# A planned order for a four-layer block, searched anew: the warm-up memset on GpSimd, other start times in the planner, another set of ranks

## The chip, the core and the metric

The kernel runs on one core of one Trainium2 chip. A core has TensorE (PE in the profile; PEld is its weight load), VectorE (DVE), ScalarE (ACT), GpSimd (POOL) and SyncE (SP), which here only issues DMAs. The metric is the device time of one execution in microseconds, the median of several runs. The profile comes from one further execution.

## The reference

Four layers follow each other on `x` (2048 rows, 512 columns, bf16): attention, gated MLP, attention, gated MLP. Each is added to `x`, and each reads the layer norm of `x`.

```python
# attention, H = 32 heads of 16; phi is a feature map, no mask
qkv = x @ wqkv ; q, k, v per head
pq, pk = q @ w_phi, k @ w_phi
phi_q = concat(softmax(pq), softmax(-pq))
phi_k = concat(softmax(pk), softmax(-pk))
kv  = sum over s of phi_k[s]^T v[s] ;  z = sum over s of phi_k[s]
o   = (phi_q @ kv) / (phi_q @ z + 1e-6) ;  return o @ wo
# MLP, F = 1376
gate = relu(x @ W_gate) ; return (gate * (x @ W_up)) @ W_down

x = x + A(layernorm(x)); x = x + B(layernorm(x))
x = x + A(layernorm(x)); x = x + B(layernorm(x))
```

Both attention layers share their weights, and so do both MLPs.

## The kernel before

The rows are cut into 16 tiles of 128 and 4 slabs of 512. All weights and `x` stay in SBUF. The kernel is written as a list of operations with an engine each, made by plain Python functions; a list scheduler then fixes the order of every engine, and the program emits that order with semaphore waits. Each engine runs its own queue strictly in order.

**Names.** A name like `K0.3` is an operation of layer 0, tile 3; layers are 0 (attention), 1 (MLP), 2 (attention), 3 (MLP). By function:

- The set-up (L497 to L608). `warm` (L500, L569) clears a small tile and multiplies it by itself 40 times on TensorE; nothing reads the product. `WkT` and `WqT` (`turn`, L578, matmuls at L585) are transposes of the key and query weights. `Wkp` and `Wqp` (`compose`, L593, L599) multiply them by the block-diagonal matrix `BD` (L572), which holds `w_phi`. "cp" is the copy of such a product from PSUM (L475 on ScalarE, L476 on VectorE).
- `ln` (L610): `stat` and `aggr` on VectorE, `ln` and `rstd` on ScalarE, `y` on VectorE (L639) or GpSimd (L638, after `nmr`), then the transpose `yT`, either a DMA on SP's queue (L653) or a matmul (L648) with a copy `yTcp`.
- `kv_tile` (L660): `K` (L671; the first tile's four matmuls are single operations, L675), two exponentials `expk` (L682), their sums `Z` (L691) or, for ten tiles of layer 0, a half-sum `Zp` on GpSimd (L687) and the rest `Zh` on VectorE (L688); the reciprocal `lZ`, `rZ`; `norm` on VectorE (L700); `V` (L709) and its copy `va`.
- `q_chunk` (L717): `Q` (L724) and two exponentials `expq` (L728).
- `kv_sums` (L736): `kv` (L744) accumulates phi_k and V over the tiles, in bursts of tiles 0-3, 4-7, 8-11, 12-13, 14, 15. `kv0.0.2` is the burst of tiles 8-11 in group 0 of layer 0, and `kv*.2` stands for that burst in all three groups. `kvs` (L752) copies the sums out.
- `attn_tile` (L761): `R` (L777, three groups), `sm` (L791), small products `p`, `den`, `coef` on GpSimd or VectorE (L798, L800, L804), `lden` and `rden` on ScalarE between them (L802, L803), `t` (L814, L819), `o` (L823, or L824 on GpSimd), the transpose `oT` (DMA at L835 or matmul at L830), `wo` (L840), and `xa` (L843), which adds to `x`.
- `glu_slab` (L849): `g` and `u` (L870), relu (L877), `h` (L878), the last 96 columns `rem` (L898), transposed by a DMA `remT` (L907). `down` (L910): `d` in two parts (L924, L926), and `xb` (L932), which adds to `x`.

**The order.** `Program.forward` (L154) simulates the five engines with a fixed duration for each operation and picks at each step, among those that can start, the one with the highest rank. The ranks are stored in the file (`RANKS`, two bytes each, as text), and so is `MOVED`, a list of operations that take the second engine they were written for. The planner lets every engine start at `START` (L53, used at L168) and takes a matmul's duration as it is given; only the first 30 warm-up matmuls are given twice the time of the others (L569). Its own constants act on the order alone: no time of theirs enters the program.

**Order around the change.** SP issues tile 0 of `x`, the key weights in two halves, two more pieces of `x`, the query weights (L559), `x` again and the value weights; GpSimd issues the rest of `x` (L565). TensorE runs 33 warm-up matmuls, the key transposes, `yT0.0`, `Wkp` with seven more warm-up matmuls in between, the four `K0.0`, and then the query transposes.

Of the kernel before, what the change touches and what calls it, by code (L numbers as in the profile page):

```python
# [12 lines left out]
P = 128  # L13

ENGINES = ("sp", "act", "pe", "dve", "pool")
# [36 lines left out]
class Program:  # L52
    SYNC, START = 40.0, 750.0  # L53
# [100 lines left out]
    def forward(self, prio, look=60.0):  # L154


        ops, SYNC = self.ops, self.SYNC
# [10 lines left out]
        free = dict.fromkeys(ENGINES, self.START)  # L168
# [32 lines left out]
        while left:  # L201
            pick = None
            for e in ENGINES:
                f = free[e]
# [4 lines left out]
                for o in ready[e]:  # L209
                    st = o.ready if o.ready > f else f  # L210
# [40 lines left out]
            if o.dma == "tr":  # L251
                free[e] = st + self.TR_ISSUE
                bus = max(bus, free[e]) + o.nbytes
                o.end = bus + self.TR_FIXED
            elif o.dma:
                free[e] = st + o.ii
                bus = max(bus, free[e]) + o.nbytes / self.DMA_BW
                o.end = bus + self.DMA_FIXED
            else:
                free[e] = st + o.ii  # L260
                o.end = st + o.lat
                if e == "pool":
                    pool_end = free[e]
                elif e == "dve" and o.port:
                    port_end = free[e]
# [155 lines left out]
def build_kernel(nc, A_x, A_wqkv, A_w_phi, A_wo, B_x, B_W_gate, B_W_up, B_W_down, out):  # L421
    pr = Program()
    op = pr.op
# [76 lines left out]
    o_warm = op("dve", lambda e: e.memset(wm.ap()[:, 0:128], 0.0), writes=[c_warm], ii=60, lat=100, name="warm")  # L500
# [67 lines left out]
    for k in range(WARM):  # L568
        op("pe", lambda e: e.matmul(pt_w.ap()[:, 0:128], wm.ap()[:, 0:128], wm.ap()[:, 0:128], start=True, stop=True), reads=[c_warm], writes=[r_w], ii=107 if k < 30 else 56, lat=300, name="warm")  # L569
# [436 lines left out]
    '!w2>Ux&|!>HwXv_1qd?;DhMbDD+qc9_XiRP1O*xhEC?V7GzjMhg8@DU@CO(O@dpP8`Uf8fA_o2kU<D`wJqUdSg#|wdY6a8><p<CQ7Y9NJ>jdTl#0MG!J_!B=',  # L1006
    'KnR`$76*_7&jq>%3JB^4r~*U?{|6BW^##`l>j&lsz6Y@civmUn)d!#i=mQ@Ivjz?VtOr>IQwJai{ssdGst2D2pa*3K<pyF0LkKwtm<L1$p#~!ebq8VvWCsZd',
    '&j$bph6Ni3sRv93Qw7=v*9PnayaxsbF$fn3A_yY~Aqb5HE(in&fd)7TF$ORQq6ZlWQU)mqI|zpd90(l+Uk6nO69}dT9SA1~a|ad({Rbon+6Ms${09#R0svSC',
    'P6s9i-Un(2I0rBX6$dW}3<x#|Ee2-?X$J=Y(+8IY4G2jG_Xb-BwFWT<3J2i@bp}TU;s(M63kT5#%m&s5QU^T;%?1t#nFSXH)CM^P&IZc{$_6I~7zbGfum)5H',
    'mj*TluLTVT$OeuE#s+5w6bN4ixd!0|O9r3@Zw7P)KL_yx*ak}gL;>gqSpr@J3<os@D+eA30R&V8t_6ArN(Z3_js@KZ0tapf?gk|YkOo)=*#?^iMF<%OHV1<S',  # L1010
    'qz17DGzR+y;|2=|+Xndug$7OrQwE|2(g%kI0tns)_y+a`fClddC<m_w=?5kV0S8tF-v*fmU<QN+R|Yx;9tY9|&ju+6MFu_xG6o3;y#*u(#|91u;0A~WbOwwD',
    'kp|}mcm_KL@CIE5sRmI74hD$^b_S&es0L{UYz8w1o(6LU1P4I|n*|yNj|K$?lm;ON!v_Bb5C<m(S_U}>V+Ldf#RtI!jRw#KPzKNh9R~FVrUdZ@PX_%4F9#t9',
    'l?Ijs&IRlSYX@To5eI4pB?o#1JO=y(9tPtFmIgcr^9Cse4+m}qIR;Dw90$<{;s=}u^93#j?FJJE83slMt_CUv(gu76BL!#%tOlG0umuVQeh1?P&<3Xk=K?1N',
    '+6CzaG6lE=>IL@&)diddsRT#`90uzK5C#+mF9tgY00y50g9ktc=LH1@*#)}?fCmi+0|xO0z6F#A%LnEK$p>@?zy%Qnat5*mng_N8?*&{3PY25dc?UHIw*`#{',
    'VFc6#M+dM6kOfo)aR-3~Z3lh^1_vMp_68;gLkFz}`Uai{Lk36&JqC~mj|Yqgvj+eOBL;T{B?e{(T?hFEe+L@~<Of9uItQ!;p9ii7YX&d|jt9R7b_d4?nFkOE',
    'r3YFE#|3x=EeA3OiU-OB`3CF<qy>`)w+Dg;-3HtT=>~)cHwVH8%?DQpl?AE>(*~9Yfd_jBO9#~kxCRmjd<3)yod<;n@dVfhwFj*SO$YM_PzSOH!UlW?h6jrW',
    'cn3@e@&{1|+XvwXA_wgU6bDoX?F1VHLIlVMUI!`%sRf${y$7cUeglUC`~{T<%m*_EZwD0!#s@(NyaNXZkq3JQ?gQinv<9^WItZ@^YzMyv_y>pwU<c?2s0Y~x',
    'k_Yq$RtG@`$_GRS?+3XDz625m<pl@?p#?|;<OZq($pp~@>IUEk9S0NzC<br`LI*zu`v<`X1O`<GNd}h(k_OiWng-4XH3X*yDh62xHwNqjG6;qSD+5Lc^#}F@',
    'X#{8m0tRmdDF&Mae+7#Ka0R~v2nN3eKnHOI$^~}^y9O)<8wT<PvIfipHU-26!v*97K?RZpV+9iiOa*WTiv>srmIZAF>jg>#P6ZDJWd>gbQU$;UW(EodO$8qY',
    'g9Y~lga!BoIt4HVNd<5OX9X_>UIW<!{R0vOX$67>O9j#d;sxphD+bX8J_X(cVg`-_H3l>Vd<A0!ECmAvy96l&Nd%k&6$HEjM+IF4b_H7ns0A$qbp%EQl?3Vp',  # L1020
    '`U9W^=mkXu;slHZPX&<#f&)MWE(DnbZ3S`#GX*3A<_07NTm}CHfdeE33IyK;#RUlluLQORSOoe7a|LDvN(03M!2|OIwghwo=>+%$-2{>Z#Reb+Bn0pTlLMCo',
    'v;?;Vh6JkvSp@wAt^}h469kh4Hw8lly93k&A_ZRry9K`k%moPqq6HcRZ3Dvt*aW=<5d@|MCj`g@(**hir3HNl2?bFFKm+~+I|Tm&Q3L}59tC{^eg#_t8U;`U',
    'Wdr*HfCZofBLoWsT?F|AwgdD9Jp!Qv!UJytiUiXEcLYfS<pf3qR|C@nR|FUZECiGT>jM!6as!71Jp(%f!31jrTmy6hTm)<cqXxDIkOPzjy#^Nr7zQ;6JP4)-',
    'Z2|@eJOrc%zz3ZMm<8Vl$p+j7UIu6biUx58*ag-H83lg^kp;2@ss()p(*<`0odsJ4-UYb@O$0&)c?N<8N(Hn9WChU#lLd(fu?4&a)dW@r%>?cT*#s^H>;?M;',
    '-~~hlbOZwj-33(z%>}Ck$pt(G$OZBSodZw>Yz3VJ6$YaPlLp%b!3J0b8wLLaZv^lK0tHnBc?GisD+CA!76ujtm<Bion*!nk90NlFh63aRUjwZIDFgQcU;-Be',
    'E(06|Zv*86ssxAw`vm&~BLkuWzX4AIgaeiW5d)V3I0O|1xdYY(QUfgo)&tiA>;en}ivzO)GXo+5zyrww5(CcyB?Suw9|JK2+61`-5CwSy$^$3^#sgXd6aygx',
    '$O7R4;{rPcbp;It?gW1XMFa)~C<Vp@#{$9xz6LA@9|ed6ZUlA&)C2AXhXwrw!vv262L{{*jReaCKL)S_69u6J#RP-|&je8ew+0Iaqyy#ztOTtDU<6JCI0a<|',
    '$O8=oi3BhNNdsmCvjvO;ECcNWDFPV-Uji5c4g}`|VFJYhvI0f|ngpi=0tCtem;+P;#sbR&@B+>P;sLe+kptNRR01FadjeJjM+6N6-vk;4p91m(-~`_T2?GuT',
    '7z6kM&jCULfdcaa8Uok@83ZB&Jp>2?fdo$jS_JX}^a79qiUMN;a{^=n3j-Acx&&tgeFB&SSpzf!Km?iv+yp-Zvjgt~xCEsGg9DBP+ygWOK?F+#as;0Q2L(3+',
    'M*|cAg9J?m5(FUyn*-<sx&_Gr-UHhM#{|v<0R=$=qy&Hjd;;|Zc?5<77X#e`T>}OKM*?938v>mIsseZdv;yV=hXSbrX9B$eIs^d&rUI@576fwxe*^XcQUoRh',  # L1030
    '?gHTf<pQ|^vI8aq{Q^w_Ed$&Fegv5Vg#yk4(gVN(69Ys8O9C4M!vWR;9s{HTS^^yd-~##rDg<!@jRRx@rvfhoe*z%{QUc-vi30=#paT8^gaWq$0|TQ3f&_^L',
    'd;>8BJOh9O;RFQ*B?AHjr34rR)&#@^cm%ow%L2CpVg$_tHUnz|dITT@HUvHc00lw?5Co3{aRn;{^aNW3Yy)Nk`~sl@ZUfr{00fN!^#eZyGy+iqXau+e^8>&H',
    '`~!Of=mPly#{<a&9|Q*j^aCXXngU`200Z^|g#%Lq?E*mpr~~-}0|c)FGXk*!zXFs3u>)fQrvrcjO9OWUIs-8SY6FM`Pyz)5wE}Dc%mN_+9t5xh1_bZ}Qv!$r',
    'kpW->sRJ(pPXyru)dN-nk^_YVkpjK~ngdn?o&yvDcmt~f-vYV<l>*8D-2(LiRRgR7(E@4$!2;C+Qvf#tP6B5ET>^dp9RPX)0s%(>UIMEGg#l>-J^~K`IRY{S',
    '=>jkUDFCen?*R<}@BnfGTm~iuTLMG`NdZa%mIEIE3IaI*0|58~IRohfZU(#sy#rbWs|R%hs05w`VFwNc4+RYYC<Jf=Xb1ELatEvfUIncKWdt+_GX#qUR|Uoe',
    'wFG1Y3<UfJdjvTI2nBirVFp7376aD;v;$KF9RWW9s{mO5s{uFzr2&rxQUJ^Z;{<yJ@c|+P&ja@Z3<eAZ!~(Sg3IlTl1q9#&G6N6;odKf<*961`q62CK2?A{d',
    '7Xq9FDgjCc0S49q@&o4t?f^&w2LwF<?FG08lmsdR^#c3>W&vgb!~-S*I02>udjZA(eFd)qq5v-gb^}!as|G^^*aDLRVFfM+iUlwOHv!%PNCI~PNB~>{C;|Qh',
    'X#=(bJq5l4n*r|xoB~Y&y8<=>q6BLNiUYg^%m8)*u?Ic`76CT|d;r}5a{w#?asZ430RWx?w*YVg3IRm|!vgUF(*pkj)B?={_yG(85&|6r&;o$~jRB4VIRP#L',
    '000&Oxd7w=xByrKLIddlCIDgrzyXy5egYH(F97EOj{?L1H3QlMP6OKlO#=b~f&w)HnE@>Vx&Zh9>H=y3m;hA)Cjtop`~b57qyeS@>;Rzw=K#q7lL3|iPXXWo',
    'WdQa8WC7O!90ETAtpT_K?*hsJ`vKAd1OqApu>h0-00NKzI|7mbrvUx{fC1S7sR7afJ^+jYUjZNjECHYa;{kF3SORAQy#fRQ5dx3_tN=U#T>ugR-vDy~qXD}C',  # L1040
    ';sCAzi2&&Ve*oJ6p8&=I!~rz{ssXM70Rry;%>lFlhXCFHrU2ytz5!SPnF81WtpE=Livh<0Kmhvyg90-FxB(^sumRcv?EzH+905!LWdaug`T=+VC;(9blmNj2',
    'rvU~6j{(R5(*XGZ{sET(hylC-oB^c(P62@dh5?!ZGyx|7eE{JAHUYE%cmcHmOamSQ+5lhyA^?K`jscngI0EDVO95yBj{w#H%K$9_E&-kZvH;Zq>H$LldI5X^',
    '*Z`jaod9_O5drG~mH=7-S^)V0YXV&X2m!YN5CLNWXaWWS&j57-4gnJYCjlh^#Q{12%>V}h^Z+CQ3jrAbi2`;3^#Dx(qX2pUm;s0YDFF`v&;VfodjNs}00A)q',
    'Py<W?^Z}Uw4+O#hIs!2P#{kX%G6MGjU;zCAMgu$oc><{b;{zcAmjhP;!U6~auL14>9Rjle!U4Si83Nk@$N-T5L;?^3k^=Ss{{bTa(E*<W1Ol)E4FV$q-T@T>',
    'UID-W1p*}k{{RO9vH|P?Q~}ZeMFVaE-vJy1TmkR_TL8rXtN{}O&;tts^8r%<QUNOh)B)rITLGg2l>s6FcL7-eKmv3Dh5#-AMFEWfqyXyz8v&{S>Hs_dD*?6u',
    'HUO9cumFq!HvmNdbpeV2BLQy#-~bl@Pyvzwr2?P;x&h?@-2r9*o&iV!&;f}7Rsn4RaRF=rZUM0YxdEF1z5wz8K>;-Y!vJXkeF0+tFabURe*shgLIFwv%K=6K',
    '6##+(&H;-6H~{7V0RapETmWzYaRLhfVgRTBZU8U<MgSlImjGx0JphCO3IL)3Cj*55Q2=WI@&J<n?EoqO1p(*)+yLkS4+1~|69J3>YXOG=B>*1+7y(xRbpVb4',
    'iU3yvZ2%qsbO7-HWB?!l3;`qpUI6O=c>vh}OaK@FoB+`PfB<Iz`T#lrNdO@Lt^hj#M*tQ80|7$;8vrW+Z~^lGVF6D7{QxuoPyna_egSa+2>=xWy8vnc5CGKx',
    'SOA0o;{f*n)BsKZ6acRPI{|C}Rsh@q83AGe%mK9k9|3Ow8UUdH9s$<?+5s8?<^e1KF9Br%l>iO^LI6Yn!2kvT2mp5gX#f!bb^yNsG5|^d1pqPuK>$Ah8~|Sc',
    'F#r+(yZ{6MGXNw2EdT',  # L1050
)
MOVED = (
    72, 74, 77, 93, 97, 101, 114, 167, 194, 303, 313, 472, 473, 476, 498, 499, 525, 528, 556, 644, 648, 652, 676, 696, 700, 717, 720, 724, 741, 748,
# [60 lines left out]
```

## Time and profile before

| | |
|---|---|
| median of 7 runs | 391.84 us (391.51 to 392.32) |
| the profiled execution | 392.14 us, its span 390.3 us |
| granted TensorE clock over the span | 1.00 |
| first matmul / last instruction's end | 1.22 us / 390.3 us |
| VectorE, ScalarE, GpSimd busy | 290.5, 198.3, 58.4 us |
| DMA transposes to landing, median | 2.5 us (55 of `y`, 28 of `o`) |

The span is from the first to the last instruction; the 1.84 us around it belong to the execution, not to the program's instructions. A row of a timeline gives start, length, engine, line, what is written from what, and a count when equal rows were merged; idle time and who ended it stand in brackets. Busy time of TensorE counts a matmul up to its modelled end, so back-to-back matmuls overlap and only distances between starts tell its pace.

### The profile page before, as it was taken

What the parts mean: (1) busy time and instruction counts of PE and PEld (TensorE: products, weight loads), DVE (VectorE), ACT (ScalarE), POOL (GpSimd) and SP (SyncE); (2) the same over time, 40 slices, a digit from 0 to 9 for tenths busy, and PEclk for the clock granted to TensorE, in tenths of its full rate; (3) what the DMA queues carried; (4) which work ended last, traced back from release to release, by engine and by line L of the source; (5) the groups of instructions that cost most, each with busy time, mean ns of one, the idle gap of its engine ahead of it and who ended that gap; (6) DMA issues with size and microseconds to landing.
All of it is one profiled execution on the core that took longest, in us unless ns stands there. A gap on an engine that the chain in (4) does not pass through costs nothing.

```text
span 390.3 us, 6693 instructions
## 1 busy us (share of the span) xinstructions
PE 380.0 (97%) x2471; PEld 213.7 (55%) x2471; DVE 290.5 (74%) x645; ACT 198.3 (51%) x617; POOL 58.4 (15%) x122
## 2 busy tenths in 40 slices
PE   7999999999999999999999999989999999999996
PEld 6545574787554544444444557567765444444443
DVE  7999978999996678335599996889989853444323
ACT  5899979665453233331269975865455313323100
POOL 2367402223320210000000000131112010000000
PEclk9999999999999999999999999999999999999999
DMA  7642941234242222100210000113233321010002
GB/s 238 177 87 55 335 141 29 53 61 65 40 82 52 44 41 42 27 0 2 53 27 16 13 3 2 28 32 71 50 68 67 55 58 37 29 40 15 1 27 81
DMA packets 60593, 22.89 MB, mean 59 GB/s; under 512 B 51761, under 2 KB 60305, under 8 KB 60561
## 3 DMA queue, kind: packets, MB, share of 16 engines
q1 hardware_dynamic: 57440, 19.35, 22.4%
q10 hardware_dynamic: 2832, 2.08, 1.7%
q0 software_dynamic: 288, 1.05, 0.8%
q8 instruction: 19, 0.31, 0.3%
q14 instruction: 14, 0.11, 0.1%
HBM read 8.44 MB, written 2.10 MB: 27 GB/s over the span
## 4 chain that ended last, share of the span: by engine, by line
PE 78%; ACT 8%; DVE 8%; DMA 4%; issue 1%; SPq 1%; POOL 0%
PE pb L870 34%; PE pb L924 17%; PE pb L840 6%; PE pb L671 4%; PE pb L709 4%; PE pb L724 3%; PE pb L744 3%; PE pb L777 3%; PE pb L898 3%; DVE phik L700 3%; ACT expq L728 3%; ACT phik L682 2%; PE pb L926 2%; DMA Wd<-in_A_wqkv_dram 2%; DVE z L688 1%; DMA oT<-o 1%
## 5 line engine op out<-in xcount | busy, mean ns | idle before, releaser
L877 ACT ACTIVATE gate<-pb 128x512 bf16<-128x512 f32 (+1 forms) x100 | 50.9, 509 | 83.8 <-PE pb L870 83.0
L878 DVE TENSOR_TENSOR hT<-gate,pb 128x512 bf16<-128x512 bf16 (+1 forms) x100 | 57.1, 577 | 41.9 <-PE pb L870 36.6
L870 PE MATMUL pb<-yT,Wu 128*128 128x512 bf16 (+1 forms) x400 | 82.7, 337 | 0.0
L870 PE MATMUL pb<-yT,Wg 128*128 128x512 bf16 (+1 forms) x400 | 81.2, 337 | 0.1
L924 PE MATMUL pb<-Wd,hT 128*128 128x512 bf16 (+2 forms) x330 | 76.6, 373 | 0.0
L870 PEld LDWEIGHTS pb<-yT,Wg 128*128 128x128 bf16 x400 | 38.5, 98 | 30.4 <-ACT gate L877 0.4
L870 PEld LDWEIGHTS pb<-yT,Wu 128*128 128x128 bf16 x400 | 38.6, 98 | 29.9 <-DVE t L814 0.2
L924 PEld LDWEIGHTS pb<-Wd,hT 128*128 128x128 bf16 x330 | 31.5, 98 | 34.8 <-DVE hT L878 0.4
L613 DVE BATCH_NORM_STATS2 stats<-x_sb 128x6 f32<-128x512 bf16 x64 | 43.4, 686 | 0.6
L932 DVE TENSOR_TENSOR x_sb<-x_sb,pb 128x512 bf16<-128x512 bf16 (+2 forms) x33 | 22.0, 668 | 28.0 <-PE pb L926 27.8
L728 ACT ACTIVATE expq<-pb 128x512 bf16<-128x512 f32 x64 | 36.1, 622 | 5.7 <-PE pb L724 5.7
L682 ACT ACTIVATE phik<-pb 128x512 bf16<-128x512 f32 x64 | 35.7, 615 | 1.7 <-PE pb L671 1.6
L814 DVE TENSOR_TENSOR t<-pb,sm 128x384 bf16<-128x384 f32 x64 | 33.9, 549 | 2.1 <-POOL sm L804 1.8
L840 PE MATMUL pb<-wo,oT 128*128 128x512 bf16 x128 | 32.6, 380 | 2.0 <-DMA oT<-o 1.3
L622 ACT ACTIVATE lnv<-mv,eps 128x1 f32<-128x1 f32 (+1 forms) x58 | 17.1, 299 | 30.5 <-DVE mv L614 30.0
L709 PE MATMUL pb<-wv,yT 128*128 128x512 bf16 x128 | 31.2, 379 | 0.0
L724 PE MATMUL pb<-yT,Wqp 128*128 128x512 bf16 x128 | 30.9, 380 | 0.2 <-DVE t L819 0.2
L671 PE MATMUL pb<-Wkp,yT 128*128 128x512 bf16 x124 | 30.2, 380 | 0.0
L639 DVE TENSOR_SCALAR y<-x_sb,mv,rstd 128x512 bf16<-128x512 bf16 x62 | 25.5, 420 | 3.9 <-ACT rstd L624 3.7
L804 POOL TENSOR_TENSOR sm<-sm 128x64 f32<-128x64 f32 x18 | 5.8, 323 | 148.5 <-ACT sm L803 148.5
L791 ACT ACTIVATE sm<-pb 128x48 f32<-128x48 f32 (+1 forms) x96 | 16.4, 221 | 21.6 <-PE pb L777 21.3
L691 DVE TENSOR_REDUCE z<-phik 128x64 f32<-128x1024 bf16 x21 | 24.8, 1203 | 0.6 <-ACT phik L682 0.6
(79 smaller groups left out, 431.5 us busy)
## 6 DMA issues: line engine op xcount, KB each, us to landing
out_dram<-x_sb ACTq DMA_DIRECT2D x15, 128.0 KB, 1.7
Wg<-in_B_W_gate_dram SPq DMA_DIRECT2D x2, 640.0 KB, 7.1
Wu<-in_B_W_up_dram SPq DMA_DIRECT2D x2, 640.0 KB, 8.1
Wd<-in_B_W_down_dram SPq DMA_DIRECT2D x1, 1280.0 KB, 11.5
x_sb<-in_A_x_dram POOLq DMA_DIRECT2D x2, 512.0 KB, 4.7
yT<-y SPq DMA_TRANSPOSE x55, 2.5
Wd<-in_A_wqkv_dram SPq DMA_DIRECT2D x2, 256.0 KB, 3.0
Wd<-in_A_wqkv_dram SPq DMA_DIRECT2D x1, 512.0 KB, 6.8
```

The lines of the kernel that those rows point to most:

```text
L613: op("dve", lambda e, t=t: e.bn_stats(stats[:, t, :], x_sb[:, t, :]), reads=[res("x", t)], writes=[res("st", t)], ii=600, lat=690, name=f" ...
L671: i = e.matmul(kt.ap(), src.ap()[:, ic, c0:c0 + 128], Wkp[:, ic, :], start=(ic == 0), stop=(ic == 3))
L682: op("act", lambda e, s=s: e.activation(ft.ap()[:, s, :], kt.ap(), ACT.Exp, scale=(1.0, -1.0)[s]), reads=[kr], writes=[fr2[s]], ii=477, la ...
L709: i = e.matmul(vt.ap(), src.ap()[:, ic, c0:c0 + 128], wv[:, ic, :], start=(ic == 0), stop=(ic == 3))
L724: i = e.matmul(qt.ap(), Wqp[:, ic, c * 128:(c + 1) * 128], src.ap()[:, ic, :], start=(ic == 0), stop=(ic == 3))
L728: op("act", lambda e, g=g: e.activation(es[g][0].ap(), qt.ap(), ACT.Exp, scale=(1.0, -1.0)[g]), reads=[qr], writes=[es[g][1]], ii=477, lat ...
L814: return e.tensor_tensor(tt_.ap()[:, b, 0:384].rearrange("p (c h d) -> p c h d", h=8, d=16), pt.ap()[:, 0:432].rearrange("p (c w) -> p c w ...
L840: i = e.matmul(wt.ap(), oT_.ap()[:, c, :], wo[:, c, :], start=(c == 0), stop=(c == 3))
L870: i = e.matmul(pt.ap()[:, 0:n], W[:, ic, fc * 128:(fc + 1) * 128], src.ap()[:, ic, a * 128:b * 128], start=(ic == 0), stop=(ic == 3))
L877: op("act", lambda e: e.activation(st_.ap()[:, 0:n], gt.ap()[:, 0:n], ACT.Relu), reads=[gr], writes=[sr], ii=110 + n * .72, lat=230 + n * ...
L878: op("dve", lambda e: e.tensor_tensor(ht.ap()[:, a * 128:b * 128], st_.ap()[:, 0:n], ut.ap()[:, 0:n], ALU.mult), reads=[sr, ur], writes=[h ...
L924: i = e.matmul(pt.ap()[:, 0:n1 - n0], hT[l, s, fc].ap()[:, c:c + 128], Wd[:, fc, n0:n1], start=(fc == 0), stop=False)
```

## The change

It has four parts.

1. The warm-up tile is cleared by GpSimd in place of VectorE. The instruction becomes a memset of 128 two-byte columns in place of 64 four-byte ones, and stands first among GpSimd's own instructions.
2. The planner gets a start time for each engine, and takes matmuls that start before 5600 ns at twice their duration; the warm-up matmuls have one duration.
3. The ranks are replaced.
4. `MOVED` is replaced.

```diff
-    SYNC, START = 40.0, 750.0
+    SYNC, CLOCK = 40.0, 5600.0
+    START = {"sp": 740.0, "act": 760.0, "pe": 400.0, "dve": 800.0, "pool": 310.0}
...
-        free = dict.fromkeys(ENGINES, self.START)
+        free = dict(self.START)
...
-                free[e] = st + o.ii
-                o.end = st + o.lat
+                slow = o.ii if e == "pe" and st < self.CLOCK else 0.0
+                free[e] = st + o.ii + slow
+                o.end = st + o.lat + slow
...
-    o_warm = op("dve", lambda e: e.memset(wm.ap()[:, 0:128], 0.0), writes=[c_warm], ii=60, lat=100, name="warm")
+    o_warm = op("pool", lambda e: e.memset(wm.ap()[:, 0:128], 0.0), writes=[c_warm], ii=60, lat=100, name="warm")
...
-        op("pe", lambda e: e.matmul(pt_w.ap()[:, 0:128], wm.ap()[:, 0:128], wm.ap()[:, 0:128], start=True, stop=True), reads=[c_warm], writes=[r_w], ii=107 if k < 30 else 56, lat=300, name="warm")
+        op("pe", lambda e: e.matmul(pt_w.ap()[:, 0:128], wm.ap()[:, 0:128], wm.ap()[:, 0:128], start=True, stop=True), reads=[c_warm], writes=[r_w], ii=55, lat=240, name="warm")
...
 RANKS = (
...
 MOVED = (
-    72, 74, 77, 93, 97, 101, 114, 167, 194, 303, 313, 472, 473, 476, 498, 499, 525, 528, 556, 644, 648, 652, 676, 696, 700, 717, 720, 724, 741, 748,
...
+    75, 79, 97, 101, 107, 191, 293, 303, 472, 473, 476, 482, 498, 499, 502, 517, 576, 580, 620, 621, 624, 668, 676, 700, 720, 740, 741, 744, 748, 765,
...
```

The ranks are numbers in a packed form; what they do is read from the order that comes out. No operation is added or dropped and every matmul keeps its shape. Of the 2,119 operations these stand differently:

- Engines. 81 operations change their engine. In the set-up and the first kv stage: three `BD` products from GpSimd to VectorE, two `WkT cp` and `yTcp0.0` from VectorE to ScalarE, one `Wkp cp` and one `Wqp cp` from ScalarE to VectorE, `y0.8` and `y0.13` from GpSimd to VectorE, `y0.12` the other way, `va0.6` from ScalarE to VectorE and `va0.8` back. Later: five `va` copies of layer 2, `oTcp0.0`, `oTcp2.0`, `yTcp1.1`, `yTcp2.15` and `yTcp3.0` from ScalarE to VectorE, `yTcp3.1` back, and 56 of the small products `p`, `den`, `coef` and `o` between VectorE and GpSimd, 33 of them to GpSimd.
- TensorE. 35 warm-up matmuls come first (33 before), then the four `WkT`, `yT0.0`, the four `Wkp`, five warm-up matmuls, three of the four `K0.0`, two `WqT`, the last `K0.0`, and the rest. `kv*.2` and what follows it end with `Q0.1.0` ahead of `R0.0.0`, where it stood behind it. Nine `K`, eight `V` and one `Q` of layer 2 run ahead of layer 1's last part `d1.14.1`; before, none did. `wo2.4` moves back behind `wo2.5`; `rem3.2.1`, `wo2.12` and `wo2.14` move too.
- DMA queues. SP's loads keep their order; the transposes follow the new order of `y`, `o` and `rem` (for layer 0: tiles 4, 5, 7, 6, 8, 9, 12, 10, 13, 11, 15, 14). GpSimd's two loads of `x` keep their place behind its sixteen small memsets.

## The prediction

> **What bounds the kernel now.** I read the page first, then busy time by stretch, then TensorE's waits, then single rows.
>
> ```profile
> PE 380.0 (97%) x2471; PEld 213.7 (55%) x2471; DVE 290.5 (74%) x645; ACT 198.3 (51%) x617; POOL 58.4 (15%) x122
> PE 78%; ACT 8%; DVE 8%; DMA 4%; issue 1%; SPq 1%; POOL 0%
> ```
>
> TensorE is the bound, and the chain that ended last is mostly TensorE. A matmul's modelled end overlaps the next one, so I count by starts: four 512-column matmuls start within 0.86 us, 0.216 each. Summed over the 2471 matmuls (0.216, 0.109, 0.0825, 0.0625, 0.058 and 0.056 us for 512, 256, 192, 144, 129 and 128 columns), TensorE's work is 374.9 us. The rest of the span is 1.22 us before the first matmul, 3.28 us from the last start to the end, and 10.95 us of stalls and slow clock in between. The work is the same after the change; only this rest can move. By stretch (each row: length, then busy time of each engine):
>
> ```profile
> 10.00:48.24 38.24, 37.59 (x252) 20.07 (x253) 37.69 (x71) 36.13 (x104) 21.87 (x30) 1.00 0.59 160
> 48.24:69.28 21.04, 19.54 (x180) 12.56 (x181) 16.53 (x43) 17.58 (x60) 3.76 (x9) 1.00 0.30 89
> 69.28:240.00 170.72, 170.72 (x1075) 95.08 (x1076) 132.64 (x277) 81.39 (x251) 16.46 (x29) 1.00 0.19 36
> 240.00:262.74 22.74, 21.05 (x160) 12.79 (x158) 20.18 (x54) 18.39 (x69) 4.76 (x13) 1.00 0.14 25
> 262.74:313.00 50.26, 50.26 (x362) 32.35 (x363) 45.48 (x118) 24.14 (x93) 7.69 (x14) 1.00 0.33 61
> ```
>
> From 69 to 240 and 263 to 313 us TensorE never rests: no order can gain there, only lose. In the first stretch VectorE (37.69 of 38.24) is as full as TensorE. What TensorE waited for:
>
> ```profile
> PE pb L585 <- DMA Wd<-in_A_wqkv_dram: 1.3, 1, 1.3
> PE pb L840 <- DMA oT<-o: 1.3, 1, 1.3
> PE pb L569 <- DVE rowi L502: 1.2, 1, 1.2
> PE pb L898 <- DMA yT<-y: 0.9, 1, 0.9
> PE pb L744 <- DVE phik L700: 0.6, 1, 0.6
> PE pb L648 <- DVE x_sb L843: 0.6, 1, 0.6
> PE pb L840 <- ACT yT L475: 0.5, 1, 0.5
> ```
>
> By starts these are, in order of the list, 1.48 us (at 10.03), 1.46 (wo2.4, at 262.74), the 1.22 at the beginning, 1.03 (rem3.2.1, at 314.32), 0.79 (kv0.0.2, at 48.24), 0.76 (yT1.0) and 0.62 (wo0.3, at 69.28). They are all that the new order can win.
>
> **Part 1: the warm-up memset goes to GpSimd.** The memset took 0.11 us on VectorE behind eight small ones; GpSimd starts at 0.74, and its 512-column memset takes 0.52, so 128 columns cost some 0.15 and the first matmul moves from 1.22 to about 0.95. Its cover:
>
> ```profile
> 1.22 3.57 PE L569 MATMUL pb<-gate 128*128 128x128 bf16 x33 [1.22 <-DVE rowi L502]
> 4.63 0.61 PE L585 MATMUL pb<-ident,Wd 128*128 128x128 bf16 x8
> 3.16 0.47 SPq L559 DMA_DIRECT2D Wd<-in_A_wqkv_dram  x1
> 7.46 1.27 PE L675 MATMUL pb<-Wkp,yT 128*128 128x512 bf16 x3
> 10.03 0.84 PE L585 MATMUL pb<-ident,Wd 128*128 128x128 bf16 x12 [1.30 <-DMA Wd<-in_A_wqkv_dram]
> ```
>
> The warm-up's 33 matmuls start 0.103 us apart, the transposes after it 0.056: the clock rose at about 4.5, 3.3 us after the first. Then everything stands until 10.03, when the query weights (issued at 3.16, 6.8 us to landing) are there. A rule speaks here: the Trainium skill, page "TensorE: Matmul & The Clock Gate", part on the clock gate, says the activity window of some 3.4 us runs free of the kernel. By it the rise may come up to 0.27 us earlier or not at all; by the row, 3.3 us after the start, it comes 0.27 earlier. If it came later, at 5.6 as the planner's new constant has it, the 20 or so real 128-column matmuls in that time would lose 0.055 each, 1.1 us, still under the 1.48 us stall at 10.03. All three give zero. The three BD products that go from GpSimd to VectorE (0.2 us each) lie before 10.03 too.
>
> One thing is not covered. The old order does all four K0.0 matmuls before 10.03; the new one puts two WqT transposes, which wait for 10.03, before the fourth. **+0.22 us** of work is left over, and ScalarE's first exponential moves from 9.06 to about 10.9.
>
> **Part 2: the first kv stage.** VectorE starts at 10.46 with the first WqT copy and does not stop until the last norm ends at 49.99. In the new order its work between these two is the same plus one Wqp copy (0.60 by starts) plus one y (y0.8 and y0.13 come from GpSimd, y0.12 goes there: 0.32): **+0.92 us**. The last norm then ends at about 50.9. GpSimd's half-sums can add to this:
>
> ```profile
> 34.22 2.44 POOL L687 TENSOR_TENSOR t<-phik 128x512 f32<-128x512 bf16 x2 [1.42 <-DVE z L688]
> 35.58 1.63 DVE L700 TENSOR_TENSOR phik<-phik,rz 128x1024 bf16<-128x1024 bf16 x1
> ```
>
> A norm that takes 0.60 took 1.56 by starts, because GpSimd ran. This happened to y0.14, norm0.6 and norm0.7, each second in line after a half-sum had freed a buffer (0.75, 0.96, 0.96). In the new order that place is taken by y0.15, y0.14 and norm0.9: three again, zero. In the new order four norms, not three, follow norm0.11, which kv*.2 waits for: it ends at 50.9 - 2.4 = 48.5. From there 3.7 us of kv matmuls and Q0.1.0 (0.86, which stood behind R0 before) lead to R0.0.0 at 53.1, against 51.95: **+1.15 us** in all, the 0.22 included.
>
> **Part 3: from R0.0.0 to slab 0 of layer 1.** Both orders have 15.1 us of TensorE work from R0.0.0 to the same place; the old one took 17.33 (51.95 to 69.28). Unstalled, the new one is there at 68.2. What is late next is the copy yTcp1.0: following ScalarE's order (21 exponentials of 0.477, four lden/rden pairs, the sm copies; one oTcp and yTcp1.1 now on VectorE) I get its end at 68.6, so rem1.0.0 at 68.7. Bounds are 68.2 and 70.4 (old stalls kept): -1.1 to +1.15. I take **-0.4** for parts 1 to 3 together, near the queue sum's -0.6.
>
> **Part 4: 69 to 240 us.** Nothing to gain. Two edges are tight. wo0.13 to rem1.3.0 has 6.5 us of TensorE work in between; xa, stat, aggr, ln, rstd, y take 2.7 us at best and the transpose 2.5, with 0.2 around the edge: 5.4, 1.1 to spare. K2.14 now ends 4.6 us ahead of kv2.1.4; its two exponentials, Z, lZ, rZ and norm take 3.9. I take **+0.3**, bounds 0 and 0.8.
>
> **Part 5: the second start, 240 to 263 us.** wo2.4 now stands 11.0 us of work behind its R2.4, not 7.1: its 1.46 us go. Late next is wo2.5, 7.9 us behind R2.5 with all four small products on GpSimd (about 2.0 us, against 0.8 on VectorE); that chain sums to 7.4. What the old stall was made of decides:
>
> ```profile
> 258.25 1.19 SPq L835 DMA_TRANSPOSE oT<-o  x1
> q8 instruction: 1, 0.02, 2.8%
> oT<-o SPq DMA_TRANSPOSE x1, 4.4
> ```
>
> The transpose took 4.4 us to land, not the usual 2.5 (median of 28), and in that stretch (259 to 262) one 16 KB instruction block went over the DMA engines; at 311 us, before rem3.2.1, it was 4.0 with a block as well. The Trainium skill, page "Runtime: NRT & Kernel Launch", section "Instruction fetch mechanics", says that blocks of 256 instructions are fetched and that the cost is mostly hidden. By the rule wo2.5 has 0.5 us to spare and the part gains 1.46; by the row a transpose issued within 2 us before a block loses 1 to 1.9. Counting matmuls between the blocks' times in this trace, they come some 124 apart, which puts one just where oT2.5 is in flight. I go by the row: 0.7 us of new stall, **-0.75**, bounds -1.46 and +0.4.
>
> **Part 6: 263 us to the end.** rem3.2.1 waited for y3.10, held up in VectorE's queue and then by a block. Now y3.10 has 23 us and y3.11 7.9, of which 5.9 are needed: **-1.03**. Places with little room are new (d3.3.1 1.4 us behind u3.0.9.2; rem3.3.1 8.2 behind wo2.14; four half-finished sums in PSUM from 334 on): **+0.6**, bounds 0 and 1.5. The tail has the same last four groups: 0.
>
> **Sum:** -0.4 + 0.3 - 0.75 - 1.03 + 0.6 = -1.3 us. The profiled execution took 392.14 (span 390.3 and 1.84 around it); it becomes 390.85. The median of the runs shown, 391.84, is 0.3 lower: **390.6 us**. The bounds add to -3.6 and +2.8; not all meet, so the forecast's own range is 389.5 to 391.2.
>
> **Rivals.** *VectorE becomes the bound of the first 50 us.* For it: 37.69 busy of 38.24 and 0.92 more to do, and y0.7 to y0.11 come 2 to 4 us later than before, with their transposes. Against it: the next part had 2.2 us of stalls to absorb it. Two more meetings with GpSimd (0.96 each) on top of 1.15, absorbed by nothing since ScalarE sets part 3, give +3.1; less some 0.9 that parts 4 to 6 save: 394.0. It decides once R0.0.0 starts after about 54.4. *Stalls only move*: as many tight places meet a block or a queue as before, each some 1 us: 391.8. For it: at most a few of the hundred transposes are critical, and which is chance. *All wins, no new stall*: -1.1, -1.46, -1.03: 388.2; against it speaks every tight edge above. That the order doesn't change is excluded: TensorE's sequence differs from the K0.0 matmuls on.
>
> **Chances.** Forecast 0.42, VectorE 0.32, only moved 0.18, all wins 0.08. What can be told from no change is about 0.2%, 0.8 us: below 391.05 is faster, above 392.6 slower. A tenth of the forecast falls inside the band: faster 0.46, same 0.21, slower 0.33. The range reaches from most of the wins to most of the VectorE case: 388.9 to 393.7.
>
> **What would show it.** First matmul near 0.95 and WqT still at about 10.0; R0.0.0 at 53.1; no stall row on L777 or L840 around 69 us; a stall at wo2.5, none at wo2.4; none at L898 near 310. I am wrong if R0.0.0 is past 54.4, or if the full stretches show stalls over 1 us.

## The result, and the profile after

The new kernel takes **389.97 us** (median of 14 runs, 389.25 to 391.46); the kernel before took 391.84 beside it (35 runs). The ratio is 0.9956, 95% interval 0.9946 to 0.9965: faster by 1.87 us, where 1.3 was forecast. The profiled execution of the new kernel took 388.88 us with a span of 387.1. It is 1.1 us under its own median, so the two profiles differ by more (3.26 us) than the medians do. One row explains the surplus: the first query transpose starts at 8.90 here and at 10.03 before, because the query weights happened to land earlier (5.7 us after their issue instead of 6.8):

```profile
8.90 0.62 PE L587 MATMUL pb<-ident,Wd 128*128 128x128 bf16 x8
```

The load stands at the same place of SP's queue in both kernels, and over all fourteen profiles of this study that transpose starts anywhere from 8.90 to 10.24, in the old and in the new start alike. I therefore count from it where I compare places.

From the page, the busy times and the chain that ended last:

```profile
PE 380.6 (98%) x2471; PEld 214.3 (55%) x2471; DVE 294.5 (76%) x646; ACT 194.9 (50%) x609; POOL 57.4 (15%) x129
PE 79%; DVE 9%; ACT 9%; DMA 1%; issue 1%; POOL 1%; SPq 0%; POOLq 0%
```

DMA has fallen from 4% of the chain to 1%. By stretch (length, then busy time of TensorE, its weight load, VectorE, ScalarE, GpSimd), with the same bounds as before:

```profile
10.00:48.24 38.24, 36.62 (x248) 19.43 (x246) 38.24 (x72) 36.67 (x105) 21.47 (x29) 1.00 0.54 149
48.24:69.28 21.04, 20.91 (x187) 13.16 (x185) 16.68 (x46) 16.17 (x59) 2.63 (x9) 1.00 0.34 104
69.28:240.00 170.72, 170.65 (x1070) 94.23 (x1069) 137.65 (x288) 79.54 (x247) 13.98 (x26) 1.00 0.19 36
240.00:262.74 22.74, 22.56 (x176) 14.59 (x175) 20.31 (x53) 18.02 (x64) 6.44 (x16) 1.00 0.16 32
262.74:313.00 50.26, 50.03 (x340) 30.54 (x338) 40.60 (x95) 20.55 (x79) 7.87 (x21) 1.00 0.28 55
```

VectorE is now busy through the whole first kv stage, 38.24 of 38.24, and TensorE lost a microsecond there; the next stretch gives it back. The fourth stretch, 21.05 of 22.74 before, is now full. TensorE's waits, in answer to the list of before:

```profile
PE pb L746 <- DVE phik L702: 1.3, 1, 1.3
PE pb L571 <- POOL expo L521: 1.0, 1, 1.0
PE pb L673 <- DMA yT<-y: 0.3, 1, 0.3
PE pb L842 <- ACT sm L793: 0.2, 1, 0.2
PE pb L601 <- DVE yT L478: 0.2, 1, 0.2
```

Lines are two higher than before. The waits of `wo` and `rem` for their DMA transposes (L842, L900; 1.3 and 0.9 us before) are gone. A kv burst waited for a norm before too (0.6 us, at `kv0.0.2`); now it waits 1.3 us, one burst earlier, at `kv0.1.1` (L702).

Cut at `R2.0.0`, the first product of the second attention layer, where both orders have done the same work (matmul counts and shapes ahead of it and behind it are equal), the picture is short:

| by starts, us | before | after |
|---|---|---|
| first query transpose to `R0.0.0` | 41.92 | 43.23 |
| first query transpose to the end of stalls around 69 (`wo0.3`, `rem1.0.0`) | 59.25 | 59.23 |
| first query transpose to `R2.0.0` | 228.53 | 228.79 |
| `R2.0.0` to the last matmul | 148.49 | 146.10 |

All of the gain lies behind 238 us. There the work is 144.64 us in both orders, and the stalls fell from 3.85 to 1.46.

### The profile page after: what moved, and what is told of

Its sections match the earlier page's. It is cut to its first block, busy times and chain, and to the rows that moved or that the text cites. A ratio compares the mean times of both kernels' runs of the same rounds, so it can differ in the third digit from the quotient of the medians.

```text
span 387.1 us, 6699 instructions
## 1 busy us (share of the span) xinstructions
PE 380.6 (98%) x2471; PEld 214.3 (55%) x2471; DVE 294.5 (76%) x646; ACT 194.9 (50%) x609; POOL 57.4 (15%) x129
## 3 DMA queue, kind: packets, MB, share of 16 engines
q0 software_dynamic: 288, 1.05, 0.8%
## 4 chain that ended last, share of the span: by engine, by line
PE 79%; DVE 9%; ACT 9%; DMA 1%; issue 1%; POOL 1%; SPq 0%; POOLq 0%
PE pb L872 33%; PE pb L926 17%; PE pb L842 6%; PE pb L726 5%; PE pb L673 4%; PE pb L711 4%; PE pb L746 3%; ACT phik L684 3%; PE pb L779 3%; PE pb L900 2%; ACT expq L730 2%; PE pb L928 2%; DVE phik L702 2%; DVE stats L615 1%; DMA x_sb<-in_A_x_dram 1%; ACT vaug L477 1%
## 5 line engine op out<-in xcount | busy, mean ns | idle before, releaser
L872 PE MATMUL pb<-yT,Wg 128*128 128x512 bf16 (+1 forms) x400 | 82.2, 337 | 0.0
L730 ACT ACTIVATE expq<-pb 128x512 bf16<-128x512 f32 x64 | 35.2, 617 | 8.9 <-PE pb L726 8.9
L842 PE MATMUL pb<-wo,oT 128*128 128x512 bf16 x128 | 32.5, 379 | 0.2 <-ACT sm L793 0.2
L641 DVE TENSOR_SCALAR y<-x_sb,mv,rstd 128x512 bf16<-128x512 bf16 x63 | 28.1, 461 | 4.0 <-ACT rstd L626 3.8
L845 DVE TENSOR_TENSOR x_sb<-x_sb,pb 128x512 bf16<-128x512 bf16 x32 | 21.8, 680 | 11.2 <-PE pb L842 11.0
```

Source lines behind the costliest of these rows:

```text
L730: op("act", lambda e, g=g: e.activation(es[g][0].ap(), qt.ap(), ACT.Exp, scale=(1.0, -1.0)[g]), reads=[qr], writes=[es[g][1]], ii=477, lat ...
L842: i = e.matmul(wt.ap(), oT_.ap()[:, c, :], wo[:, c, :], start=(c == 0), stop=(c == 3))
L872: i = e.matmul(pt.ap()[:, 0:n], W[:, ic, fc * 128:(fc + 1) * 128], src.ap()[:, ic, a * 128:b * 128], start=(ic == 0), stop=(ic == 3))
```

## The experiments

My theory was that two late DMA transposes made the old stalls at `wo2.4` and `rem3.2.1`, and that each was late because a 16 KB block of TensorE's instructions was fetched just behind it. The rival was that the chains were late in the old order by themselves, and a second rival was that part of the gain comes from the start. Twelve kernels were run. Ratios are to the kernel before on the same chip (its median lay between 391.49 and 391.90 there); the last two columns are by starts from the profiles, as in the table above. In some traces a few dozen matmul records are missing, which moves none of these starts.

| kernel | median, us | ratio, 95% interval | to `R2.0.0` | behind it |
|---|---|---|---|---|
| before | 391.84 | 1 | 228.53 | 148.49 |
| after | 389.97 | 0.9956 [0.9946, 0.9965] | 228.79 | 146.10 |
| old to 238 us, then new | 389.67 | 0.9957 [0.9945, 0.9968] | 228.59 | 146.26 |
| new to 238 us, then old | 391.84 | 0.9997 [0.9981, 1.0014] | 228.75 | 148.18 |
| old, memset on GpSimd | 392.02 | 1.0009 [0.9995, 1.0022] | 228.75 | 148.58 |
| old, +40 instructions | 389.98 | 0.9959 [0.9947, 0.9971] | 228.62 | 146.39 |
| old, +120 | 392.21 | 1.0007 [0.9997, 1.0018] | 228.54 | 148.84 |
| old, +255 | 391.57 | 0.9995 [0.9977, 1.0012] | 229.23 | 147.95 |
| new, +40 | 389.84 | 0.9943 [0.9922, 0.9965] | 228.76 | 145.72 |
| new, +120 | 390.76 | 0.9972 [0.9962, 0.9981] | 228.74 | 146.96 |
| new, +228 | 391.00 | 0.9976 [0.9960, 0.9993] | 228.77 | 147.19 |
| new, VectorE relieved | 389.77 | 0.9942 [0.9921, 0.9962] | 228.47 | 146.35 |
| new, relieved, +40 | 389.72 | 0.9940 [0.9925, 0.9955] | 228.50 | 145.71 |
| old to 238, then new, +40 | 389.41 | 0.9945 [0.9929, 0.9962] | 229.03 | 145.72 |

### Where the gain lies: two halves joined

The planner's sequence was cut behind the last `kv` product of the second attention layer, and each operation kept the engine of its half. The first version has the old front, the second the new one.

```diff
     pr.schedule(ROUNDS, ranks, MOVED)
+    pr.replay(_u16(ORDER), _u16(SLOTS))   # old order up to the last kv2 product, then the new one
```

> The old order and engines up to the last kv matmul of the second attention layer (238 us), the new ones from there on. Theory (all of the gain lies behind 240 us: the new order gives wo2.4 and rem3.2.1 more room): 2.0 to 2.5 us under the kernel before, as good as the new kernel or up to 0.3 better, with no stall of over 0.5 us behind 240 us. Rival (part of the gain comes from the first 70 us, as one profile with the query weights landing 1.1 us earlier suggests): only 0.8 to 1.3 us under the kernel before.

> The new order and engines up to the last kv matmul of the second attention layer, the old ones from there on. Theory (gain only behind 240 us): 0 to 0.4 us over the kernel before, with the stalls at wo2.4 (1.5 us) and rem3.2.1 (1.0 us) back, unless the 16 KB instruction blocks, whose places depend on how many instructions TensorE has had, now fall elsewhere. Rival (the first 70 us gain): 0.8 to 1.3 us under the kernel before.

Measured: 0.9957 and 0.9997. The old front with the new back is as fast as the new kernel, the new front with the old back is the old kernel. In TensorE's waits of the second version both old rows stand again (lines moved by the added function):

```profile
PE pb L859 <- DMA oT<-o: 1.3, 1, 1.3
...
PE pb L917 <- DMA yT<-y: 0.7, 1, 0.7
```

By starts they are 1.42 us at `wo2.4` and 0.90 at `rem3.2.1`. So the first 238 us give nothing that can be measured, and everything of the change that counts is behind them. My expectation for the first version was wrong in one detail: a stall of 0.55 us remained at `wo2.6`.

### The memset alone

```diff
     pr.schedule(ROUNDS, ranks, MOVED)
+    o_warm.eng = "pool"
+    pr.sequence.remove(o_warm)
+    pr.sequence.insert(0, o_warm)
```

> The kernel before with only the clearing of the warm-up tile moved to GpSimd, everything else in place. Theory (covered by the wait for the query weights): first matmul at 1.0 instead of 1.22, the first query transpose when the weights land, time within 0.3 us of the kernel before. Rival (the earlier warm-up makes the clock rise earlier and helps the first 10 us): 0.5 to 1.1 us faster.

Measured: 1.0009 [0.9995, 1.0022]. The timeline of TensorE in this version starts (start, length, engine, line, operation, count, idle before):

```profile
1.00 3.70 PE L569 MATMUL pb<-gate 128*128 128x128 bf16 x33 [1.00 <-POOL expo L519]
4.50 1.06 PE L585 MATMUL pb<-ident,Wd 128*128 128x128 bf16 x8
```

The first matmul is at 1.00 instead of 1.22, the first query transpose at 10.00. Eight key transposes take 1.06 us where the old profile had 0.61: the clock rose later here (at 5.8 us) than before (4.5), and it cost nothing, because the query weights were not there: TensorE still waited 0.95 us for them. The memset is worth nothing.

### Only the blocks moved: the old order with 40 more instructions

TensorE's order, engines and tiles are untouched. Two waits that are always met go ahead of each of forty `g` and `u` operations of layer 1; two waits fit into one instruction, so these are 40 instructions, or 20 matmuls' worth (a matmul is two, with its weight load), not the 30 to 40 matmuls of my expectation.

```diff
+            for k in range(2 if e == "pe" and o.name[:5] in ("g1.2.", "u1.2.", "g1.3.", "u1.3.") else 0):
+                eng.wait_ge(sems["dve"], k + 1)
             ins = o.fn(eng)
```

> The kernel before with its order untouched and 80 waits that are always met put on TensorE between 90 and 200 us, so that all later 16 KB instruction blocks are fetched some 30 to 40 matmuls (about 5 us) earlier. Theory (the two late stalls were made by DMA transposes that were issued just ahead of such a block): oT2.4 and y3.10 land in 2.5 instead of 4.35 and 4.0 us, the stalls of 1.46 at wo2.4 and 1.03 at rem3.2.1 go, 1.5 to 2.5 us under the kernel before with no change of order. Rival (the chains were late in the order itself, and blocks only happen to be near): within 0.3 us of the kernel before, stalls still there; if the waits themselves cost, slower.

Measured: 0.9959 [0.9947, 0.9971]. **The old order with forty instructions that do nothing is as fast as the new kernel.** The view of the DMA queues from 256.5 to 259.5 us of this version, in which oT2.4 (issued at 257.66) lands:

```profile
q8 instruction: 1, 0.02, 1.9%
issues: line engine op xcount, KB each, median us to landing
oT<-o SPq DMA_TRANSPOSE x1, 2.4
```

The block (q8) of before's 260.2 us is fetched at 257.4, ahead of the transpose, and the transpose takes 2.4 us instead of 4.4. The timeline of TensorE has no bracket at `wo2.4` and at `rem3.2.1`:

```profile
260.90 0.81 PE L842 MATMUL pb<-wo,oT 128*128 128x512 bf16 x3
...
311.64 0.82 PE L900 MATMUL pb<-Wr,yT 128*128 128x192 bf16 x8
```

The first rival falls here: with an unchanged order, the stalls of 1.46 and 1.03 us go when the blocks move. A new one of 0.40 us came at a `wo` product at 272.8.

### Moved by a whole block: the old order with 255 more

To exclude that the waits themselves help, a whole block's length was added, so that behind 205 us the blocks fall where they fell before.

```diff
+            for k in range(6 if e == "pe" and (o.name[:5] in ("g1.1.", "u1.1.", "g1.2.", "u1.2.", "g1.3.", "u1.3.", "d1.4.", "d1.5.", "d1.6.", "d1.7.", "d1.8.", "d1.9.", "d1.10", "d1.11", "d1.12", "d1.13", "d1.14", "d1.15") or o.name == "K2.5") else 0):
+                eng.wait_ge(sems["dve"], k + 1)
             ins = o.fn(eng)
```

> The kernel before with 255 more instructions on TensorE between 105 and 205 us, in place of the 40 of the shifted one: a block holds 256, so behind 205 us the blocks fall again where they fell in the kernel before, only one earlier in number. Theory (the place of the blocks made the stalls): oT2.4 and y3.10 take about 4 us again, the stalls at wo2.4 (1.2 to 1.5 us) and rem3.2.1 (0.9 to 1.5 us) are back, time within 0.4 us of the kernel before. Rival (the extra waits themselves did it, for example by spacing TensorE's instructions): as fast as the shifted one or faster, 1.5 us or more under the kernel before.

Measured: 0.9995 [0.9977, 1.0012]. With six times as many added instructions the gain is gone. Blocks come at 260.9 and 311.8, oT2.4 takes 3.95 us, y3.10 3.86, and TensorE stands at `wo2.4` again:

```profile
263.15 1.02 PE L842 MATMUL pb<-wo,oT 128*128 128x512 bf16 x4 [0.89 <-DMA oT<-o]
```

By starts the two stalls are 1.05 and 0.89 us. Between 100 and 238 us, where the waits were put, TensorE's stalls stay at or under 0.03 us per 10 us, as without them: waits that are met cost nothing there.

### Half a block: both orders with 120 more

The same edit as the shift by 40, with six waits in place of two.

```diff
-            for k in range(2 if e == "pe" and ...
+            for k in range(6 if e == "pe" and ...
```

> The kernel before with 120 more instructions on TensorE between 130 and 195 us: blocks 60 matmuls earlier, half the way to the next. The two old stalls should go; the block that came at 260.2 us now comes near 251, where oT2.2 and oT2.3 are issued (249.1, 251.3) and wo2.3 has 0.3 us to spare. Theory: 2.5 us less of stalls and 0 to 1.6 more at wo2.2 or wo2.3, 0.9 to 2.4 us under the kernel before. Rival (any shift helps alike): as the shift by 40, 1.6 us under.

> The new kernel with 120 more instructions on TensorE between 130 and 195 us: the block of 258.6 us now comes near 250.5, 1.4 us behind the issue of oT2.2 (249.1). Theory: oT2.2 takes about 4 us, wo2.2 (at 251.9, oT2.2 usually there at 251.6) stalls 1.0 to 1.5 us, the 0.39 us at wo2.6 goes: 0.6 to 1.1 us over the new kernel. Rival (the new order is safe for most places of the blocks): within 0.4 us of the new kernel.

Measured: 1.0007 for the old order, 0.9972 for the new. In the old order the blocks come at 253.2 and 269.5, and two other transposes are hit: oT2.3 (issued at 251.5, 3.97 us) and oT2.5 (267.1, 4.46). TensorE waits for both:

```profile
255.62 1.02 PE L842 MATMUL pb<-wo,oT 128*128 128x512 bf16 x4 [1.34 <-DMA oT<-o]
...
271.60 1.69 PE L842 MATMUL pb<-wo,oT 128*128 128x512 bf16 x7 [1.31 <-DMA oT<-o]
```

I had allowed for the first and not for the second, so I expected a gain and got none: the two old stalls had gone and two new ones of 1.5 us had come. The rival, that any shift helps alike, fell with it. In the new order the block fell at 253.6, later than I had counted, and met oT2.3 (4.09 us), not oT2.2; the stall of 1.32 us is at `wo2.3`. Its row shows how the view can mislead:

```profile
255.97 1.02 PE L844 MATMUL pb<-wo,oT 128*128 128x512 bf16 x4 [1.16 <-DVE mv L618]
```

The bracket names a small VectorE operation, the one whose event came last by the profile; the transpose that took 4.09 us landed at 255.84, and `wo2.3` followed.

### The new order: a block put where oT2.5 flies, and 40 more

```diff
+            for k in range(6 if e == "pe" and o.name[:5] in ("g1.1.", "u1.1.", "g1.2.", "u1.2.", "g1.3.", "u1.3.", "d1.4.", "d1.5.", "d1.6.", "d1.7.", "d1.8.", "d1.9.", "d1.10", "d1.11") else 0):
+                eng.wait_ge(sems["dve"], k + 1)
             ins = o.fn(eng)
```

> The new kernel with 228 more instructions on TensorE between 105 and 190 us, which puts a block 14 matmuls later than it was, to about 259.8 us, 1.1 behind the issue of oT2.5. Theory (the prediction's stall at wo2.5 failed to come because no block met oT2.5): oT2.5 now takes about 4 us, wo2.5 stalls 0.7 to 1.6 us, oT2.4 and oT2.6 are back at 2.5 us; 0.4 to 1.2 us over the new kernel, 0.7 to 1.5 under the kernel before. Rival (the new order has room enough at wo2.5): no stall over 0.4 there, as the new kernel.

> The new kernel with 40 more instructions on TensorE between 130 and 195 us, so that blocks come 20 matmuls earlier. Theory: oT2.6 is no longer hit (4.0 us to 2.5), the 0.39 us at wo2.6 goes and nothing comes: 0.2 to 0.5 us under the new kernel, 2.1 to 2.4 under the kernel before. Rival (that stall comes from the order): as the new kernel, 1.9 under the kernel before.

Measured: 0.9976 [0.9960, 0.9993] with 228 more, 0.9943 [0.9922, 0.9965] with 40 more. In the first the block comes at 261.7, 1.7 us behind oT2.5's issue at 260.0 (all is some 1.3 us later than in the new kernel's profile, as the query weights landed later). oT2.5 takes 4.11 us, and `wo2.5` stands 1.48:

```profile
264.21 1.02 PE L844 MATMUL pb<-wo,oT 128*128 128x512 bf16 x4 [1.31 <-DMA oT<-o]
```

So the room at `wo2.5` is as small as the prediction had it, and the new kernel was spared only because its block came at 258.6, 0.04 us before oT2.5 was issued, and not a microsecond or two behind it. With 40 more the stall at `wo2.6` (0.39 in the new kernel, where oT2.6 took 4.0 us with a block 1.9 behind it) goes, although oT2.6 still takes 2.9 us, with a block 0.38 behind it; the part behind `R2.0.0` is 145.72, as short as in any version. In time this can't be told from the new kernel: the intervals overlap.

### VectorE's load in the first kv stage

```diff
+    alone = {o.i: (o.eng, o.fn) for o in pr.ops}
     pr.schedule(ROUNDS, ranks, MOVED)
+    for i in (107, 194):                 # the Wqp copy, y0.13
+        o = pr.ops[i]
+        o.eng, o.fn = alone[i] if i == 107 else o.alt[:2]
```

> The new kernel with the Wqp copy that moved to VectorE back on ScalarE and y0.13 back on GpSimd, which takes 0.92 us from VectorE in the first kv stage. Theory (VectorE sets the end of that stage, ScalarE the next one, which takes up the difference): counted from the first query transpose, R0.0.0 0.4 to 0.9 us earlier, rem1.0.0 within 0.3 us of the new kernel, time within 0.3 us of it. Rival (VectorE's extra 0.92 us costs the whole kernel): 0.6 to 0.9 us under the new kernel. If ScalarE is as full as VectorE there, R0.0.0 doesn't move.

Measured: 0.9942 [0.9921, 0.9962], 389.77 us, not to be told from the new kernel. `R0.0.0` comes 0.31 us forward (42.92 behind the first query transpose; 43.17 to 43.23 in the five profiles that have the new front unchanged), and the 0.3 us are still there at `R2.0.0` (228.47 against 228.74 to 228.79). So the difference isn't taken up later, and only a third of the 0.92 us shows. VectorE's own starts say why. From its first `WqT` copy to the start of its last norm it took 39.53 us here and 39.77 in the version "new to 238 us, then old", which has the same front without the relief. The two operations (0.60 and 0.32) are gone, but three others took longer: y0.10 0.58 instead of 0.32, the remaining Wqp copy 0.75 instead of 0.60, norm0.3 0.86 instead of 0.60. The first of them ran beside y0.13, which GpSimd had just got back (the second row is y0.10 and the `y` after it):

```profile
25.02 0.77 POOL L640 TENSOR_SCALAR y<-x_sb,rstd,nmr 128x512 bf16<-128x512 bf16 x1
25.27 0.98 DVE L641 TENSOR_SCALAR y<-x_sb,mv,rstd 128x512 bf16<-128x512 bf16 x2
```

The edit thus took only 0.24 us from VectorE, and `R0.0.0` moved by about as much: the run does not show that VectorE's load counts for a third. TensorE's wait for the norms shrinks only a little:

```profile
PE pb L746 <- DVE phik L702: 1.1, 1, 1.1
```

### Joined

> The new kernel with both the copy and y0.13 taken from VectorE and the 40 more instructions on TensorE. Theory (the two are independent: 0.3 us in the first 50 us, 0.4 at wo2.6): 0.4 to 0.8 us under the new kernel, 2.3 to 2.7 under the kernel before, from R2.0.0 to the last matmul 145.7 us. Rival (no more to be had from either): as the new kernel.

> The old order up to 238 us, the new one from there, and the 40 more instructions on TensorE. Theory: as the version with relief, 2.2 to 2.7 us under the kernel before, R2.0.0 some 228.5 us behind the first query transpose (228.8 in the new kernel), no stall over 0.3 us behind 238 us. Rival (the block places differ by some instructions and one still meets oT2.4, oT2.5 or oT2.6 where it counts): 1.2 to 1.9 under the kernel before.

Measured: 0.9940 [0.9925, 0.9955] and 0.9945 [0.9929, 0.9962]. Both have the 145.7 us behind `R2.0.0`. The first should have been clearly better; in its profile the end took 4.35 us from the last matmul's start instead of 3.3, since a block came at 385.1 and the last two stores took 3.3 and 3.1 us instead of 1.6 and 1.5:

```profile
out_dram<-x_sb ACTq DMA_DIRECT2D x1, 96.0 KB, 3.3
out_dram<-x_sb SPq DMA_DIRECT2D x1, 32.0 KB, 3.1
```

The second had `R2.0.0` 0.5 us later than hoped; in its profile one transpose in the first stage (issued at 15.96) took 3.17 us. No version beats the new kernel by more than the intervals.

## Why the prediction was right, step by step

Counted from the first query transpose, the profiles say 0.0 us to the place around 69, +0.28 from there to `R2.0.0`, -1.73 in the second start (the 26 us from `R2.0.0` on), -0.66 behind it: -2.1, where the steps had -0.4, +0.3, -0.75 and -0.43.

- **Part 1, zero: right**, and shown by the memset alone. One reading in it was wrong. I took from the row that the clock rises 3.3 us after the first matmul, so 0.27 earlier; the rule of the Trainium skill (page "TensorE: Matmul & The Clock Gate", part on the clock gate: the window runs free of the kernel) is the one that the runs agree with. The first matmul was at 1.00 or 1.22 in all fourteen profiles, and the clock rose anywhere from 4.17 to 7.06 us; in the new kernel at 5.8. The cover was enough each time, but it is not fixed: TensorE waited 0.34 to 1.48 us for the query weights in twelve profiles (0.53 where the clock rose at 7.06), and only 0.04 us in the new kernel's own and 0.01 in one other, where they landed early. The `WqT` transposes "still at about 10.0" were at 8.90 in this one profile, by chance of the load, and at 9.60 to 10.21 in the six others with the new front.
- **Part 2, +1.15 at `R0.0.0`: right**, +1.31, and for the reason given. VectorE's last norm ended 0.99 us later (40.96 against 39.97 behind the first query transpose; 0.92 was forecast), and the meetings with GpSimd cost the most at y0.15, y0.14 and norm0.9, as forecast. The wait itself stood one burst earlier than forecast: `kv0.1.1` waited for norm0.7, and `kv0.1.2` started 0.13 us after norm0.11 had ended.
- **Part 3, -0.4 for the three parts: 0.0.** From `R0.0.0` to `rem1.0.0` 16.0 us passed where 15.6 were counted. The edge was the right one: the copy `yTcp1.0` on ScalarE was the last to come, but it ended 59.17 us behind the first query transpose, 0.6 later than the prediction's 68.6 had it. No stall stands at L779 or L842 around 69, as said.
- **Part 4, +0.3: right** in size, +0.28, but not at the two edges named: 0.24 of it is one stall before a `u` product at 106.3.
- **Part 5, -0.75: the term of 0.7 us for a new stall at `wo2.5` failed**; without it, and with 0.3 less of small stalls, the part gave -1.73. (The seven waits listed were not quite "all that the new order can win": 0.45 us at `wo2.1` stood in the old order too.) The mechanism was right and the place missed by little: the block came at 258.62, just ahead of oT2.5 (issued at 258.66) instead of behind it. Put behind it by 228 instructions, it cost 1.48 us. It met oT2.4 instead, and `wo2.4` didn't wait, because it stands later in the new order: that step held. The view of the DMA queues from 256.5 to 258.64 us of the new kernel, and its row of `wo2.4`, without a bracket:

```profile
q8 instruction: 1, 0.02, 2.7%
oT<-o SPq DMA_TRANSPOSE x1, 4.0
...
263.17 1.03 PE L842 MATMUL pb<-wo,oT 128*128 128x512 bf16 x4
```

- **Part 6, -1.03 and +0.6: right in the first term, 0.2 too much in the second.** The new stall was at `wo2.6`, from a block again, and not at the places I had named.
- **The rivals.** VectorE as the bound was to decide from `R0.0.0` at 54.4 on; it was at 52.13, and at 53.2 to 53.4 in three runs where the query weights landed at the old time. "Stalls only move" is what the old order does at most places of the blocks that were tried.

So the mechanism held, and the sum came out near partly by luck: part 3 was 0.4 too hopeful, parts 5 and 6 together 1.2 too cautious.

In weighing the row against the skill's sentence on fetched blocks (page "Runtime: NRT & Kernel Launch", section "Instruction fetch mechanics": mostly hidden), the row was right. TensorE itself does not stop at a block (between 100 and 238 us of the kernel before six blocks were fetched, and its stalls are at most 0.03 us per 10 us), but a DMA that it waits for is held up.

What the order itself brings, apart from the luck of the blocks, is the difference at equal shifts, by starts from one profile each: behind `R2.0.0`, 2.4 us without a shift, 1.9 at +120, 0.7 at +40. The new order was shorter at each of the three, but three are few, and 0.7 us is all that it keeps where the blocks suit the old one.

## What to carry to other kernels

When a stall of one or two microseconds hangs on a single DMA that took 4 us where its like take 2.5, look at what else went over the DMA engines in those two microseconds before changing the order. If it is an instruction block, a few idle instructions further ahead move it, and a shift by a block's length tells cause from coincidence. A searched order that gains half a per cent should be timed at several shifts: part of its gain can belong to where the blocks happened to fall, and any later edit of the instruction count may take it away.

## What the runs showed of the hardware

Over the fourteen profiles there are 85 DMA transposes behind whose issue a 16 KB instruction block began 0.4 to 2.1 us later. All 85 took longer than the usual 2.47 us: 2.94 to 4.52, median 3.75, and more the later the block came (median 3.35 at 0.4 to 0.8 us, 4.03 at 1.6 to 2.1). The edges of that stretch are drawn from these profiles themselves: of the 18 with a block less than 0.4 us behind, eleven took over 2.8 us, and of the 51 with one 2.1 to 3 us behind, four. Of the 1056 with no such block from 1 us ahead of their issue to 3 us behind it, 65 took over 2.8 us. An 8 KB instruction block of another queue (q14 in the profile) began 0.4 to 2.1 us behind 73 of the 1056, and 50 of the 65 slow ones are among these. That moving the block moves the delay is shown by the shifts; why the transpose's landing waits for the block was not tried.

The clock's rise was the other surprise: 3.0 to 5.8 us after the first matmul, with nothing in the kernels that goes with it.
